# Feature group 1 of the gated branch by seven products on two chunks, and three moves around it

## The chip, the cores and the metric

The kernel runs on one core of one Trainium2 chip. The metric is the device time of one execution in microseconds. A core has five engines that each take their own list of instructions in order: PE (TensorE, matrix products into PSUM banks), ACT (ScalarE), DVE (VectorE), POOL (GpSimd) and SP (SyncE, which here only issues DMA transfers; ACT and POOL issue some too). The lists wait for each other through semaphores.

## The reference

Everything is float32. The input is 2048 positions of 640 features.

```python
xn = _layernorm(x)                        # over the 640 features
s = attention(xn)                         # 32 heads of 20; W = 8 keys at distances 0, 2, .., 14
g = silu(((xn @ w_gate) * (xn @ w_up)) @ w_down)     # 640 -> 1536 -> 640
return x + s * g
```

The attention takes q, k and v from xn @ wqkv (640 to 1920), masks keys before position 0, takes a softmax over the 8 keys and multiplies by wo (640 to 640).

## The kernel before, in words

**Products.** A float32 operand is split into a high part (a rounded copy, made by ACT, line 114) and a low part (the rest, a subtraction, line 115, on POOL or DVE), and a product is the sum of three: high by high, high by low, low by high. So 128 features against a chunk of 512 positions with 640 = 5 x 128 inputs takes 15 matmuls of 128x512.

**Gate and up.** The 1536 features are 12 groups of 128 (`f`), the 2048 positions 4 chunks of 512 (`ch`). For groups 0 and 1 the kernel does the plain thing, `gate_up(f, ch)` (line 642): 15 matmuls for gate, 15 for up, and DVE multiplies the two. For groups 2 to 10, `group(f, c0)` (line 1253) treats gate and up of two chunks (`c0`, `c0 + 1`) as a 2 by 2 block product and does it with seven block products (a scheme of Strassen's kind): 7 x 6 matmuls for four fifths of the inputs, and 4 x 3 plain ones for the last fifth. It needs sums of the weights (`w_add`: S1, S2, S3, S4, d5), their splits (`w_split`: sets G, S, R and U) and sums of the inputs (T1 to T4, made by `differences` for chunks 2 and 3, by `early_sums` and `early_high` for chunks 0 and 1).

Inside a group the products come in the order j = 0, 5, 2, 1, 4, 3, 6 (line 1285), here called n0 to n6. Products 0, 2, 4 and 6 add up in one PSUM bank (A), 1 and 3 in a second (C), 5 in a third (B). After j = 0, 1, 2 and 4 the running sum is copied out by ACT (`hold`, line 1261) before the next product adds to that bank. n0 and n1 read the weights of set G, n2 to n4 those of S (n3 also U), n5 those of R, n6 those of U.

**What is prepared when.** The raw weights of group f + 1 are loaded (`load_wf`, line 180, 640 KB) while group f runs, their sums and splits stand at places of group f (`places`, filled from `two_places`): for a full group of two halves (chunks 2 and 3, then 0 and 1) the sums at n5, n6 of the first half and n0, n1 of the second, the splits G, S, R, U at n2, n4, n5, n6 of the second half. The raw weights and the sums share two buffers (`wraw`), so that a load waits for the split that last reads the buffer.

**Order of the program.** A start stage (layer norm, transposes, q/k/v of the first head group for positions of both parities, `gate_up` of groups 0 and 1); then q/k/v of the other head groups m = 1 to 4, two times 8 tiles each (line 1356, `qkv`, PSUM copied out by ACT at line 448); then the groups; then wo, then w_down and the result. Attention's elementwise work (DVE: products L542 and L508, sums L549; POOL: the additions of L514; ACT: exponential L571 and a copy of q L498) is a generator that `advance(budget)` feeds piece by piece into the lists, at so many microseconds of credit per stretch of PE's work. In `values` (line 500) the eight weighted keys w = 0 to 7 of a unit go through two buffers in turn: the addition for w = 1 reads both, so the product for w = 2 has to wait for it. When a unit's additions are done, `store_o` (line 582) sends its result out on SP.

The number `VEC` decides on which engine the last additions of a group's first half are done (line 1257): DVE from group VEC on.

## Time and profile before

| what | value |
|---|---|
| runs | median 736.25 us of 3 (735.91 to 736.73) |
| the profiled execution: its time | 736.29 us |
| its span, first to last instruction | 734.4 us |
| PE busy | 728.2 us (99%) |
| DVE, POOL, ACT busy | 626.5 (85%), 450.5 (61%), 302.2 (41%) us |
| granted clock | 1.000 |

In the timelines a row holds its start, its length, engine, line, operation, what it writes and reads, and the count of equal instructions merged; in brackets stands the idle time ahead of it and who ended it. Times are from the span's start. A matmul row of PE reaches past the start of the next one, since matmuls overlap; the distance of starts tells what they cost.

### The profile page before, as it was taken

Reading aid. Unit: us, or ns where it says so; the run is one execution under the profiler, and the core shown is the slowest. Engines: PE = TensorE matmul, PEld = TensorE weight load, DVE = VectorE, ACT = ScalarE, POOL = GpSimd, SP = SyncE. Lnnn points to the kernel's source line nnn. Section 1 sums busy time; section 2 is a strip of 40 time slices with the busy share of each in tenths; the row PEclk is TensorE's granted clock in tenths of the full one; section 3 lists DMA queues with packets and bytes.
Section 4 is the critical chain, followed back from the end, with each engine's and each line's share of the span. In section 5 each row is a group of like instructions: output and inputs, shape, how many; then the busy total and the mean of one; then the engine's idle time right before and its main releaser. Section 6 shows DMA issues by size and latency. Waiting matters only on the chain.

```text
span 734.4 us, 11062 instructions
## 1 busy us (share of the span) xinstructions
PE 728.2 (99%) x4030; PEld 666.0 (91%) x4030; DVE 626.5 (85%) x729; ACT 302.2 (41%) x561; POOL 450.5 (61%) x383
## 2 busy tenths in 40 slices
PE   8999999999999999999999999999999999999997
PEld 6989989988999998888888888888999999999997
DVE  7676998798796989899889999969899997777775
ACT  5668312323232333333233322334566664444442
POOL 6159919997779889797879969766644550000000
PEclk9999999999999999999999999999999999999999
DMA  8564588789767669462733542376768965555534
GB/s 325 170 204 158 208 303 300 239 256 257 190 193 164 220 204 323 141 180 87 221 88 105 177 141 68 80 218 183 208 211 241 315 236 194 194 194 194 194 108 143
DMA packets 106148, 143.78 MB, mean 196 GB/s; under 512 B 23048, under 2 KB 75524, under 8 KB 106094
## 3 DMA queue, kind: packets, MB, share of 16 engines
q1 hardware_dynamic: 88366, 121.13, 52.0%
q10 hardware_dynamic: 16000, 12.78, 5.4%
q0 software_dynamic: 1728, 9.18, 5.1%
q8 instruction: 31, 0.51, 0.3%
q14 instruction: 23, 0.19, 0.1%
HBM read 94.40 MB, written 55.67 MB: 204 GB/s over the span
## 4 chain that ended last, share of the span: by engine, by line
PE 98%; DMA 1%; DVE 0%; SPq 0%; ACT 0%; issue 0%
PE g L1292 16%; PE u L1292 11%; PE q L434 11%; PE q L866 9%; PE u L434 8%; PE g L434 8%; PE u L866 6%; PE q L1292 5%; PE u L124 5%; PE g L124 5%; PE q L996 3%; PE g L866 3%; PE e L866 3%; PE u L996 2%; PE e L996 2%; PE g L996 1%
## 5 line engine op out<-in xcount | busy, mean ns | idle before, releaser
L514 POOL TENSOR_TENSOR o<-o,t 128x960 f32<-128x960 f32 (+1 forms) x66 | 133.7, 2025 | 11.3 <-DVE t L508 10.1
L508 DVE TENSOR_TENSOR t<-e,kv 128x960 f32<-128x960 f32 (+1 forms) x96 | 99.6, 1038 | 21.1 <-POOL o L514 21.1
L542 DVE TENSOR_TENSOR t<-q,kv 128x1920 f32<-128x1920 f32 (+1 forms) x48 | 92.4, 1926 | 2.8 <-DMA kv<-qkv_scr 2.7
L549 DVE TENSOR_REDUCE lg<-t 128x96 f32<-128x1920 f32 (+1 forms) x48 | 92.3, 1923 | 0.2
L434 PE MATMUL q<-s,xc 128*128 128x360 f32 (+1 forms) x450 | 82.8, 334 | 0.5 <-DVE lg L272 0.5
L1261 ACT ACTIVATE gh<-g 128x512 f32<-128x512 f32 x57 | 34.2, 600 | 109.0 <-PE g L1292 108.1
L434 PEld LDWEIGHTS q<-s,xc 128*128 128x128 f32 x450 | 74.8, 188 | 4.6 <-DVE lg L272 0.7
L115 POOL TENSOR_TENSOR s<-wraw,s 128x384 fp32r<-128x384 f32 (+6 forms) x57 | 68.0, 1209 | 17.5 <-ACT s L114 17.5
L434 PE MATMUL u<-s,xc 128*128 128x360 f32 (+1 forms) x360 | 65.8, 334 | 0.0
L434 PEld LDWEIGHTS u<-s,xc 128*128 128x128 f32 x360 | 60.3, 188 | 2.3
L434 PE MATMUL g<-s,xc 128*128 128x360 f32 (+1 forms) x330 | 61.5, 337 | 0.0
L434 PEld LDWEIGHTS g<-s,xc 128*128 128x128 f32 x330 | 55.7, 188 | 2.6
L1292 PE MATMUL g<-s,s 128*128 128x512 f32 x228 | 57.9, 389 | 0.0
L1292 PE MATMUL u<-xc,s 128*128 128x512 f32 x228 | 57.9, 389 | 0.0
L866 PE MATMUL q<-xc,s 128*128 128x320 f32 x342 | 55.5, 309 | 0.0
L866 PEld LDWEIGHTS q<-xc,s 128*128 128x128 f32 x342 | 51.5, 188 | 0.0
L1292 PEld LDWEIGHTS g<-s,s 128*128 128x128 f32 x228 | 42.8, 188 | 8.9
L1292 PEld LDWEIGHTS u<-xc,s 128*128 128x128 f32 x228 | 42.8, 188 | 8.9
L114 ACT ACTIVATE s<-wraw 128x384 fp32r<-128x384 f32 (+6 forms) x58 | 32.6, 581 | 29.4 <-PE g L1292 10.2
L1292 PE MATMUL q<-xc,pk 128*128 128x512 f32 x171 | 41.9, 389 | 0.0
L1292 PE MATMUL g<-xc,s 128*128 128x512 f32 x171 | 41.9, 389 | 0.0
L514 POOL TENSOR_TENSOR o<-t 128x960 f32<-128x960 f32 (+1 forms) x11 | 22.1, 2011 | 27.4 <-DVE t L508 22.7
(328 smaller groups left out, 1559.7 us busy)
## 6 DMA issues: line engine op xcount, KB each, us to landing
h_scr<-gh SPq DMA_DIRECT2D x48, 256.0 KB, 2.8
wraw<-in_wgu SPq DMA_DIRECT2D x11, 640.0 KB, 4.8
kv<-qkv_scr SPq DMA_DIRECT2D x14, 480.0 KB, 6.1
t<-h_scr SPq DMA_DIRECT2D x8, 768.0 KB, 6.3
qkv_scr<-s ACTq DMA_DIRECT2D x17, 360.0 KB, 4.4
kv<-qkv_scr SPq DMA_DIRECT2D x14, 367.5 KB, 7.1
s_scr<-gh SPq DMA_DIRECT2D x16, 320.0 KB, 3.6
gh<-s_scr SPq DMA_DIRECT2D x16, 320.0 KB, 4.1
```

The costliest lines, as they stand in the source:

```text
L114: nc.scalar.activation(hi, raw, AF.Copy)
L115: eng.tensor_sub(lo, raw, hi.bitcast(F32))
L124: nc.tensor.matmul(acc, a, b, start=first and n == 0, stop=last and n == len(runs) - 1)
L434: nc.tensor.matmul(p, xT[(r * NE + i) // TPC][a][:, k, t0:t0 + P], wq[m][b][k], start=n == 0, stop=n == len(runs) - 1, skip_group_check=ac ...
L508: nc.vector.tensor_mul(t.rearrange("p (n d) -> p n d", d=DH), e[:, :, w].unsqueeze(2).to_broadcast([P, NE * nh, DH]), v)
L514: return NE * c * cost, lambda: eng.tensor_add(y, z, t)
L542: nc.vector.tensor_mul(t, q, k)
L549: nc.vector.tensor_reduce(out=lg[:, :, j:j + 2].rearrange("p n a -> p a n"), in_=t.rearrange("p a (n d) -> p a n d", d=DH), op=ALU.add, ax ...
L866: nc.tensor.matmul(p, y[:, i, k], wd_part(name, k, l), start=new and r == 0, stop=r == len(runs) - 1, skip_group_check=True)
L996: nc.tensor.matmul(b, y, w, start=new and r == 0, stop=r == len(runs) - 1, skip_group_check=True)
L1261: nc.scalar.activation(kept[j], b["ACACABA"[j]], AF.Copy)
L1292: nc.tensor.matmul(y, w, x, start=j in (0, 1, 5) and r == 0, stop=r == len(runs) - 1, skip_group_check=True)
```

## The change

- `F_TWO` is 1: group 1 of chunks 2 and 3 goes through `group(1, 2)`, first of the groups, and the two plain calls `gate_up(1, 2)` and `gate_up(1, 3)` are gone. (Group 1 of chunks 0 and 1 stays plain.) The raw weights of group 1 are loaded a second time for it.
- This first group has only one half, so it has its own places (`one_places`), at which group 2 is prepared within that half. `VEC` is 1, the late loads of chunk 0 and 1's sums are spread differently, and a condition at n6 is widened.
- In the start stage the split of q/k/v weights 1, the load of weights 2 and `early_high(1)` stand after tile 5 of the second parity, in that order; `early_high(1)` came before the split, and the load of weights 2 at the start of m = 1.
- `store_o` stands after the exponential instead of ahead of the mask.
- The credit per head and tile in the q/k/v loop is 0.39 instead of 0.38.

```diff
-VEC = 2
+VEC = 1
...
             ahead(n + 1, (0,))
-            if before is not None:
-                store_o(before)
...
             finish_piece()
             yield 0.5
+            if before is not None:
+                store_o(before)
...
-    early_high(1)
...
     for i in range(TPC, NE):
         qkv(0, 1, i)
         advance(PACE * 1.9)
-    split_wq(1, nc.gpsimd)
-    gate_up(1, 2)
+        if i == TPC + 1:
+            split_wq(1, nc.gpsimd)
+            load_wq(2, ((0, 2), (2, 4)))
+            early_high(1)
     gate_up(0, 3)
-    gate_up(1, 3)
+    wf_raw.clear()
...
-    F_TWO = 2
+    F_TWO = 1
...
-            if (second, n) == (1, 6) and (second, n) in places:
+            if n == 6 and (second, n) in places and (second or f == F_TWO):
                 places.pop((second, n))(f)
...
-            advance(PACE * heads * 0.38)
+            advance(PACE * heads * 0.39)
...
-    w_split(2, "R")
-    w_sum.pop(2)
-    load_wf(3)
+    w_split(F_TWO, "R")
+    w_sum.pop(F_TWO)
+    load_wf(F_TWO + 1)
...
-    for f in range(2, f1):
+    one_places = {(0, 2): splits("G"), (0, 3): sums("S1", "S2", "S3"), (0, 4): splits("S"),
+                  (0, 5): lambda f: (w_add(f + 1, "d5", "S4"), w_split(f + 1, "R")), (0, 6): splits("U")}
+    for f in range(F_TWO, f1):
         places.clear()
-        places.update(two_places)
+        places.update(two_places if f > F_TWO else one_places)
         if f == F_TWO:
-            for n, at in enumerate((0, 2, 3, 4)):
+            places[0, 0] = lambda f: load_late(0)
+        elif f == F_TWO + 1:
+            for n, at in enumerate((0, 2, 4), 1):
                 places[0, at] = lambda f, n=n: load_late(n)
         group(f, 2)
-        group(f, 0, 1)
+        if f > F_TWO:
+            group(f, 0, 1)
```

ACT at the start of the groups, of the change. The first two rows split sets R and U of group 1 (`s_193`); `gh` rows are the holds; `wraw_194` is the raw weight tile of group 2, `wraw_201` its sums; `pk_190` is set G, `s_181` set S; the rows L569 and L498 belong to attention.

```order
L114 ACTIVATE s_193_2555<-wraw_172_2205 128x384 [waits Pool_49]
L114 ACTIVATE s_193_2555<-wraw_168_2141 128x384
L1262 ACTIVATE gh_197_2570<-g_195_2560 128x512 [waits PE_49]
L1262 ACTIVATE gh_199_2594<-g_195_2560 128x512 [waits PE_49]
L114 ACTIVATE pk_190_2501<-wraw_194_2558 128x640 [waits DMAHW6_49,Pool_49]
L1262 ACTIVATE gh_200_2609<-u_196_2561 128x512 [waits PE_49]
L1262 ACTIVATE gh_202_2623<-g_195_2560 128x512 [waits PE_49]
L114 ACTIVATE s_181_2368<-wraw_201_2611 128x768 [waits Pool_49]
L114 ACTIVATE s_193_2555<-wraw_201_2611 128x384 [waits PE_49,Activation_49,Pool_49]
L114 ACTIVATE s_193_2555<-wraw_194_2558 128x384 [waits PE_49,Activation_49]
L569 ACTIVATE e_3_70<-lg_188_2463 128x256 [waits DVE_49]
L498 ACTIVATE q2_2_69<-q_192_2549 128x640 [waits DMAHW0_49]
```

The same place before, from the split of R and U of its first group (group 2) on:

```order
L114 ACTIVATE s_202_2645<-wraw_182_2301 128x384 [waits Pool_49]
L114 ACTIVATE s_202_2645<-wraw_179_2235 128x384
L1261 ACTIVATE gh_206_2660<-g_204_2650 128x512 [waits PE_49]
L571 ACTIVATE e_3_70<-lg_191_2458 128x256 [waits DVE_49]
L498 ACTIVATE q2_2_69<-q_197_2552 128x640 [waits DMAHW7_49]
L1261 ACTIVATE gh_210_2687<-g_204_2650 128x512 [waits PE_49]
L1261 ACTIVATE gh_212_2701<-u_205_2651 128x512 [waits PE_49]
L1261 ACTIVATE gh_214_2713<-g_204_2650 128x512 [waits PE_49]
L1261 ACTIVATE gh_218_2757<-g_216_2749 128x512 [waits PE_49,Pool_49]
L1261 ACTIVATE gh_220_2790<-g_216_2749 128x512 [waits PE_49,Pool_49]
L114 ACTIVATE pk_199_2595<-wraw_203_2648 128x640 [waits DMAHW1_49,Pool_49]
```

The first split of the next group's weights (`pk` from the tile just loaded) stood behind six holds, and stands now behind two; the other three splits stand ahead of the next group's first hold.

POOL at the same place, of the change. `o_185` rows are attention's additions; the first row is the low part of set G of group 1, the two `s_193` rows those of R and U.

```order
L115 TENSOR_TENSOR pk_190_2501<-wraw_168_2141,pk_190_2501 128x640
L514 TENSOR_TENSOR o_185_2442<-t_77_926 128x640
L514 TENSOR_TENSOR o_185_2442<-o_185_2442,t_77_926 128x640 x2
L115 TENSOR_TENSOR s_193_2555<-wraw_172_2205,s_193_2555 128x384
L115 TENSOR_TENSOR s_193_2555<-wraw_168_2141,s_193_2555 128x384
L1149 DMA s_198_2572<-t_scr_111 128x1536
L514 TENSOR_TENSOR o_185_2442<-o_185_2442,t_77_926 128x640 x2
L115 TENSOR_TENSOR pk_190_2501<-wraw_194_2558,pk_190_2501 128x640
L1239 TENSOR_TENSOR wraw_201_2611<-wraw_194_2558 128x256
L1239 TENSOR_TENSOR wraw_201_2611<-wraw_201_2611,wraw_194_2558 128x256
L1239 TENSOR_TENSOR wraw_201_2611<-wraw_194_2558 128x256
L514 TENSOR_TENSOR o_185_2442<-o_185_2442,t_77_926 128x640
```

And before:

```order
L115 TENSOR_TENSOR pk_199_2595<-wraw_179_2235,pk_199_2595 128x640
L514 TENSOR_TENSOR o_189_2439<-o_189_2439,t_77_942 128x640 x3
L115 TENSOR_TENSOR s_202_2645<-wraw_182_2301,s_202_2645 128x384
L115 TENSOR_TENSOR s_202_2645<-wraw_179_2235,s_202_2645 128x384
```

The three additions between the splits were the last three of a unit (w = 5, 6, 7); now they are the first three of the next (w = 1, 2, 3; the row that writes `o` from `t` alone is w = 1). Behind them POOL now has the whole preparation of group 2 in a row: split G, three sums, an addition, split S (`s_181`), two sums, split R, an addition, split U.

On SP the load of group 2's raw weights, `wraw_194`, stands behind the loads of attention's next unit and waits for POOL's low part of R, which reads the buffer last; before, the load of group 3's weights waited for the same row of group 2.

14 lines of the change are left out of this document (7 added, 7 removed).

## The prediction

> **What bounds the kernel now.** I read the page's first part, then PE's waits, then the timelines of PE, ACT, POOL, DVE and SP where the groups begin.
>
> ```profile
> span 734.4 us, 11062 instructions
> PE 728.2 (99%) x4030; PEld 666.0 (91%) x4030; DVE 626.5 (85%) x729; ACT 302.2 (41%) x561; POOL 450.5 (61%) x383
> ...
> PE q L229 <- POOL lg masks.py:199: 1.4, 1, 1.4
> PE q L434 <- DVE lg L272: 0.5, 1, 0.5
> ```
>
> The last two rows are all the waits that PE has, and both lie in the start stage. From there on PE's matmuls alone set the time: a matmul less is time won, and any wait of PE is time lost, since nothing later is idle that could give it back.
>
> ```profile
> 85.00 3.56 PE L124 MATMUL g<-xc,s 128*128 128x512 f32 x15
> ...
> 105.40 2.56 PE L434 MATMUL q<-s,xc 128*128 128x360 f32 x15
> ...
> 272.60 1.52 PE L1292 MATMUL g<-xc,pk 128*128 128x512 f32 x6
> 273.96 2.20 PE L1292 MATMUL q<-xc,pk 128*128 128x512 f32 x9
> 276.00 1.52 PE L1292 MATMUL g<-s,s 128*128 128x512 f32 x6
> 277.36 1.52 PE L1292 MATMUL u<-s,s 128*128 128x512 f32 x6
> 278.72 0.84 PE L1292 MATMUL u<-xc,s 128*128 128x512 f32 x3
> 279.40 1.52 PE L1292 MATMUL g<-s,s 128*128 128x512 f32 x6
> 280.76 2.20 PE L1292 MATMUL u<-xc,s 128*128 128x512 f32 x9
> 282.80 2.20 PE L1292 MATMUL g<-xc,s 128*128 128x512 f32 x9
> 284.84 1.52 PE L1292 MATMUL g<-xc,pk 128*128 128x512 f32 x6
> ```
>
> From 85.00 to 105.40 stand three plain gate_up calls, 90 matmuls in 20.40 us, 0.227 us each. From 272.60 to 284.84 stands one half group, n0 to n6, 54 matmuls in 12.24 us, the same 0.227 us.
>
> **What is removed.** Two plain calls of 30 matmuls become one half group of 54: 6 matmuls, 6 x 0.227 = **1.36 us**. Were nothing else to happen, the profiled time of 736.29 us would become 734.93. All other work is on other engines, and costs only what PE comes to wait. So I look at the new half group, whose start on PE I call 0; in the run before, 0 is 272.60. Without waits n2 ends at 4.76, n3 at 6.80, n4 at 8.16, n6 at 12.24, and n1 of the group after it at 12.24 + 3.40 = 15.64.
>
> **What is added: one chain.** The change's lists show it. Group 2's raw weights can only be loaded when POOL has made the low part of R of group 1. ACT's split G of group 2 waits for that load and stands *ahead* of the hold of n3's bank, to which n5 adds; and the splits S, R and U stand ahead of the first hold of group 2, without which its n2 may not add. ACT starts its rows in the order of its list, so each hold waits for all that stands before it.
>
> When is R ready? These are the rows before, for the same place of the program (the first is the copy of the last head group's tile 13, 0.47 long after 1.93 of waiting for PE: a tile takes PE 2.40; all of this hangs on PE's position, so I shift it by 13.60 with PE).
>
> ```profile
> 268.00 0.47 ACT L448 ACTIVATE s<-g 128x360 f32<-128x360 f32 x1 [1.93 <-PE g L434]
> ...
> 269.07 0.74 ACT L114 ACTIVATE pk<-wraw 128x640 fp32r<-128x640 f32 x1 [0.60 <-ACT s L448]
> ...
> 273.87 0.94 ACT L114 ACTIVATE s<-wraw 128x384 fp32r<-128x384 f32 x2 [0.60 <-ACT s L448]
> 274.71 0.58 ACT L1261 ACTIVATE gh<-g 128x512 f32<-128x512 f32 x1
> 275.19 0.38 ACT L571 ACTIVATE e<-lg 128x256 f32<-128x256 f32 x1
> 275.50 0.70 ACT L498 ACTIVATE q<-q 128x640 f32<-128x640 f32 x1
> ...
> 259.91 1.56 POOL L514 TENSOR_TENSOR o<-t 128x640 f32<-128x640 f32 x1
> 262.42 1.57 POOL L514 TENSOR_TENSOR o<-o,t 128x640 f32<-128x640 f32 x1 [0.94 <-DVE t L508]
> ...
> 264.62 1.56 POOL L514 TENSOR_TENSOR o<-o,t 128x640 f32<-128x640 f32 x1
> ...
> 269.89 1.57 POOL L115 TENSOR_TENSOR pk<-wraw,pk 128x640 fp32r<-128x640 f32 x1 [1.59 <-ACT pk L114]
> 271.42 4.88 POOL L514 TENSOR_TENSOR o<-o,t 128x640 f32<-128x640 f32 x3
> 276.24 2.02 POOL L115 TENSOR_TENSOR s<-wraw,s 128x384 fp32r<-128x384 f32 x2
> ...
> 229.79 0.39 ACT L571 ACTIVATE e<-lg 128x256 f32<-128x256 f32 x1 [2.11 <-DVE lg L569]
> ...
> 261.51 0.82 DVE L508 TENSOR_TENSOR t<-e,kv 128x640 f32<-128x640 f32 x1 [1.70 <-POOL o L514]
> ...
> 277.30 0.35 SPq L180 DMA_DIRECT2D wraw<-in_wgu x1
> ```
>
> POOL's low part of G waited for ACT, hence for PE, and ended at 271.46, that is -1.14. Three additions followed back to back (4.88), then R, and SP issued the load at 277.30 = +4.70. The change has three additions in the same gap, so **+4.7 is the early bound** of the issue, T. But they are now w = 1, 2, 3, and w = 2's product may start only after w = 1's addition. The rows of such a trio are at 259.91, 262.42 and 264.62: with DVE's wait (261.51) and a 0.62 us DMA issue between them they took 6.27 us from the first start to the last end. From -1.14 that is +5.1, R takes 1.0, and T = **+6.2**. I take this, since it is the same trio; the late bound is DVE behind by the longest that ACT's exponential waited for it in the q/k/v loop's rows, 2.11 us (229.79), so +8.3.
>
> What then has to pass until group 2's first hold is done? The prices:
>
> ```profile
> DMA to landing us min/median/max: 4.5/4.5/4.5
> ...
> 283.34 0.73 POOL L1238 TENSOR_TENSOR wraw<-wraw 128x256 f32<-128x256 f32 x1
> 284.15 1.07 POOL L1238 TENSOR_TENSOR wraw<-wraw,wraw 128x256 f32<-128x256 f32 x1
> ...
> 286.97 1.61 POOL L1238 TENSOR_TENSOR wraw<-wraw 128x256 f32<-128x256 f32 x2
> 288.55 0.74 POOL L1238 TENSOR_TENSOR wraw<-wraw,wraw 128x256 f32<-128x256 f32 x1
> ...
> 293.06 1.56 POOL L514 TENSOR_TENSOR o<-o,t 128x640 f32<-128x640 f32 x1
> 294.61 1.85 POOL L115 TENSOR_TENSOR s<-wraw,s 128x768 fp32r<-128x768 f32 x1
> ```
>
> Landing 4.5 (the load at 277.30); split G, ACT's start to POOL's end, 271.46 - 269.07 = 2.4; S1, S2, S3: 0.8 + 0.8 + 0.8 = 2.4; the addition that POOL's list has ahead of split S 1.6; split S 1.85; d5 and S4 some 1.3; ACT's R and U 0.94; the exponential and the copy of q 1.0 (275.19 to 276.20); the hold 0.58. Sum **16.5**. The hold is done at T + 16.5 and PE wants it at 15.64, so PE loses T + 0.9: 5.6 at the early bound, **7.1** at +6.2, 9.2 at the late one. It is lost in two places: the hold of n3's bank ends at T + 4.5 + 0.74 + 0.58 = +12.0 against 8.16, some 3.9 us ahead of n5, and the other 3.2 us ahead of n2 of group 2.
>
> **The edits that I cost at nothing.** The added sums, splits and holds of group 1 itself lie in the q/k/v loop behind PE, as group 2's did. The earlier m = 1 (13.60 us) needs weights 1 split by 91.8 on PE:
>
> ```profile
> 80.61 1.30 POOL L608 TENSOR_TENSOR kv<-kv,xc 128x512 f32<-128x512 f32 x1
> ...
> 89.61 4.39 POOL L115 TENSOR_TENSOR s<-wraw,s 128x1080 fp32r<-128x1080 f32 x3
> ...
> 109.50 2.27 POOL L514 TENSOR_TENSOR o<-t 128x960 f32<-128x960 f32 x1 [14.80 <-DVE t L508]
> ```
>
> The split now follows POOL's 80.61 row and is done near 82 + 4.4 = 86.4; `early_high(1)`, between those rows at 7.7 us, comes after it and ends near 94, in what was POOL's idle 14.80 us. Without that cover it would delay the split to 94, and PE by about 2 us. It does delay SP: a q/k/v store now stands behind its stores, so attention's second unit starts some 4 us later (94 against 89.6 for the last of them). That costs DVE, not PE: ACT's copy of q waits for it and holds up five banks' worth of copies, 5 x 2.4 = 12 us. The moved `store_o` waits for POOL's addition as it did. The credit of 0.39 brings 26 x 16 x 0.01 = 4.2 us of attention forward, against 13.0 of credit that the two calls no longer give and 9.9 that the half group does; DVE's share by group 2 is as before within 1 us. Price of all these if wrong: 1 to 3 us of PE's time.
>
> **Forecast.** 736.29 - 1.36 + 7.1 = 742.0 us; the profiled time is 0.04 above the median, so it stands for both. Its own range goes by the bounds of T, 740.5 to 744.1.
>
> **Rivals.** *The load is early enough*, and the change does what its matmuls say: 734.9, a shade under 0.2% faster, which is about what a measurement of this kernel can tell from no change. It decides from T = -0.9 on. Against it: ACT's split of R, ahead of POOL's, waits in its list for the last tile's copy and started at 273.87 = +1.27. For it: only that I read the order of the holds right from lists, without times. *Only the first wait stays*, if POOL's sums are covered better than I count: 736.29 - 1.36 + 3.9 = 738.8. *The early stage costs too*: the late unit and its copy on ACT add 1 to 3 us, 743 to 745. *The clock falls after the pauses.* The granted clock is 1.000 here, with no wait of PE over 1.4 us, so no row shows what a 3 to 4 us pause does. If PE ran at half clock afterwards for as long as it paused, the first loss would vanish in the second wait, which does not hang on PE; the second would cost 3.2 / 2 = 1.6 us: 743.6.
>
> [...]
>
> **How the numbers follow.** Forecast 0.64, no wait 0.12, first wait only 0.08, early stage 0.08, clock 0.08. The range 737.0 to 746.5 takes in all but the no-wait case and the tails, about 0.82. Faster by over 0.2% is half of the no-wait case, 0.06; within 0.2% the other half and a little of the small waits, 0.08; slower 0.86.
>
> **What would show it.** PE's waits of the changed kernel should have ACT's holds (L1262) as releasers, some 4 us ahead of n5 and some 3 us ahead of n2 of group 2; the load of `wraw` should be issued some 6 us after the half group's start, and ACT should idle for DMA `wraw` ahead of split G. I am wrong if PE passes 259.0 to 275 without a wait, if T lies under 3, or if PE waits in m = 1.

## The result, and the profile after

The changed kernel takes **754.09 us** (median, 753.88 to 754.64) against 736.08 for the kernel before beside it: a ratio of 1.0245, 95% interval 1.0227 to 1.0262. It is 18 us slower. The prediction said 742.0, range 737.0 to 746.5: the direction was right, the size too small by 12 us. (One run of `b_36` and one of `b_wsum8`, its profiled one, took 1037.71 and 1037.48 us at a mean granted clock of 0.655, and stand in no number below.)

First the page of the changed kernel: its span, the busy time of the engines, and the first rows of PE's waits (engine, line, who was waited for: us in total, times, longest; the rest of them, 5.6 us, are in the places below or in the start stage).

```profile
span 752.0 us, 11077 instructions
PE 734.3 (98%) x4024; PEld 666.9 (89%) x4024; DVE 628.2 (84%) x731; ACT 305.4 (41%) x568; POOL 456.2 (61%) x392
...
PE u L1293 <- POOL s L115: 2.9, 2, 2.1
PE u L1293 <- ACT gh L1262: 2.7, 2, 2.0
PE g L1293 <- POOL pk L115: 2.1, 3, 1.4
```

Before, PE waited 1.9 us, all in the start stage. Now the new waits make some 11 us of the 17.6 by which the span grew, and PE is busy 6 us longer with 6 matmuls fewer. So part of the time is not waiting: PE itself was slower for a while. The starts of the first matmul of each stage give the whole account (a "half" is one half group, seven products; the column of differences adds up to the span's).

| stretch, us | before | after | difference |
|---|---|---|---|
| start to the first product of m = 1 | 105.40 | 91.81 | -13.6 |
| q/k/v loop, m = 1 to 4 | 167.20 | 170.98 | **+3.8** |
| half group 1 (new) | none | 20.07 | 12.24 **+ 7.8** |
| half group 2 | 12.24 | 13.43 | **+1.2** |
| half groups 3 to 20, over 12.24 each | 0 | 6.2 | **+6.2** |
| what follows the groups | 229.28 | 229.23 | 0 |

Saved 13.6 and spent 12.24 are the 1.36 us of the six matmuls. Against them stand 19.0 us in three places.

**The first half group.** PE, ACT, POOL and SP of the changed kernel, from each one's timeline:

```profile
262.79 1.19 PE L1293 MATMUL g<-xc,pk 128*128 128x512 f32 x4 [0.32 <-ACT pk L114]
...
272.57 0.50 PE L1293 MATMUL u<-xc,s 128*128 128x512 f32 x1 [2.14 <-POOL s L115]
276.71 4.21 PE L1293 MATMUL u<-xc,s 128*128 128x512 f32 x9 [1.98 <-ACT gh L1262]
280.71 2.31 PE L1293 MATMUL g<-xc,s 128*128 128x512 f32 x9
...
287.31 1.66 PE L1293 MATMUL g<-s,s 128*128 128x512 f32 x6 [0.89 <-ACT gh L1262]
```

```profile
262.00 0.74 ACT L114 ACTIVATE pk<-wraw 128x640 fp32r<-128x640 f32 x1 [3.95 <-DMA kv<-qkv_scr]
...
275.43 0.74 ACT L114 ACTIVATE pk<-wraw 128x640 fp32r<-128x640 f32 x1 [6.18 <-DMA wraw<-in_wgu]
276.07 0.58 ACT L1262 ACTIVATE gh<-u 128x512 f32<-128x512 f32 x1
...
264.34 1.56 POOL L514 TENSOR_TENSOR o<-t 128x640 f32<-128x640 f32 x1
266.85 1.57 POOL L514 TENSOR_TENSOR o<-o,t 128x640 f32<-128x640 f32 x1 [0.94 <-DVE t L508]
269.04 1.57 POOL L514 TENSOR_TENSOR o<-o,t 128x640 f32<-128x640 f32 x1 [0.62 <-DVE t L508]
270.56 1.95 POOL L115 TENSOR_TENSOR s<-wraw,s 128x384 fp32r<-128x384 f32 x2
...
271.58 0.35 SPq L180 DMA_DIRECT2D wraw<-in_wgu x1
```

This is the predicted chain. The trio of additions took 264.34 to 270.6, 6.3 us; the load of group 2's raw weights was issued at 271.58, 8.8 us after the start; ACT idled 6.18 us for it with the hold of n3's bank behind (276.07), and PE waited 1.98 us ahead of n5 (276.71). PE waited 0.89 more ahead of n2 of group 2. One wait is there that the prediction does not have: 2.14 us in n3 (272.57) for POOL's low part of U, the second of the two rows at 270.56, which stands behind the same trio and behind R. The load does not hang on it, so it does not move n5; but it is a pause of PE.

What no row of before could show is the row at 276.71: nine matmuls that take 4.0 us to the next start, where they took 2.04. The windows view shows why (stretch, length, PE busy and matmuls, granted clock, DMA share and GB/s):

```profile
270.62:274.03 3.41, 1.46 (x6) 1.00 0.38 113
274.03:277.44 3.41, 1.43 (x4) 0.50 0.83 283
277.44:280.86 3.42, 3.42 (x10) 0.50 0.09 32
```

The granted clock was 0.50 for 6.8 us, two stretches of 3.41, behind stretches in which PE worked 1.46 and 1.43 us of 3.41.

**The q/k/v loop.** The stretch around its one wait of PE, of PE, SP, POOL and ACT:

```profile
185.74 2.74 PE L434 MATMUL q<-s,xc 128*128 128x360 f32 x15 [0.96 <-ACT s L448]
...
254.91 2.63 PE L434 MATMUL g<-s,xc 128*128 128x360 f32 x15
257.38 2.63 PE L434 MATMUL u<-s,xc 128*128 128x360 f32 x15
...
167.59 1.51 SPq L422 DMA_DIRECT2D kv<-qkv_scr x2
169.27 0.34 SPq L414 DMA_DIRECT2D q<-qkv_scr x1
...
168.62 0.79 POOL L768 DMA_DIRECT2D w_scr<-w_scr x1
...
181.73 3.33 ACTq L452 DMA_DIRECT2D qkv_scr<-pk x2
185.11 0.57 ACT L448 ACTIVATE s<-q 128x480 f32<-128x480 f32 x1 [8.63 <-PE u L434]
```

ACT's store of q/k/v belongs right behind its copy at 175.9 and was issued at 181.73, which took 3.3 us; for 8.63 us ACT copied nothing out, and PE waited 0.96 us for its next copy. But the loop lost 3.8. The rest is in the two rows of PE below that wait: tiles of 360 columns start 2.47 us apart from here to the end of the loop, where before, and up to this wait, they started 2.40 apart. Thirty tiles make 2.1 us. Another 0.5 lies at the end of the loop, where the groups' first split comes late. The granted clock is 1.00 there.

**The later half groups** lose 0.1 to 2.0 us in five of them, by two kinds of wait. One of the first kind, at 391 us, from ACT's and PE's timelines, and one of the second, at 436 us, from POOL's and PE's:

```profile
391.24 0.50 ACT L569 ACTIVATE e<-lg 128x384 f32<-128x384 f32 x1 [1.77 <-DVE lg L567]
...
392.57 0.58 ACT L1262 ACTIVATE gh<-u 128x512 f32<-128x512 f32 x1
...
393.20 2.12 PE L1293 MATMUL u<-xc,s 128*128 128x512 f32 x8 [0.73 <-ACT gh L1262]
```

```profile
434.04 2.27 POOL L514 TENSOR_TENSOR o<-o,t 128x960 f32<-128x960 f32 x1
...
437.86 0.73 PE L1293 MATMUL g<-xc,pk 128*128 128x512 f32 x2 [1.44 <-POOL pk L115]
```

In the first, attention's exponential stands in ACT's list ahead of the hold that PE needs next, and it waited 1.77 us for DVE. In the second, one of attention's additions stands in POOL's list ahead of the low part of split G (from 436.27) that PE reads. By the releasers of PE's waits half groups 10 and 13, 2.4 us, are of the first kind, and 4 and 14, 3.7 us, of the second.

### The profile page after: what moved, and what is told of

Same layout as the page of the kernel before. It is cut to its first block, busy times and chain, and to the rows that moved or that the text cites. A ratio compares the mean times of both kernels' runs of the same rounds, so it can differ in the third digit from the quotient of the medians.

```text
span 752.0 us, 11077 instructions
## 1 busy us (share of the span) xinstructions
PE 734.3 (98%) x4024; PEld 666.9 (89%) x4024; DVE 628.2 (84%) x731; ACT 305.4 (41%) x568; POOL 456.2 (61%) x392
## 4 chain that ended last, share of the span: by engine, by line
PE 80%; DVE 6%; POOL 5%; issue 3%; DMA 3%; ACT 1%; SPq 0%; ACTq 0%; POOLq 0%; DVEq 0%
PE g L1293 10%; PE q L434 9%; PE q L866 8%; PE u L1293 7%; PE u L434 7%; PE g L434 6%; PE u L866 6%; PE u L124 4%; PE g L124 4%; PE q L1293 3%; PE q L996 3%; PE g L866 3%; PE e L866 3%; PE u L996 2%; POOL o L514 2%
## 5 line engine op out<-in xcount | busy, mean ns | idle before, releaser
L514 POOL TENSOR_TENSOR o<-o,t 128x960 f32<-128x960 f32 (+1 forms) x66 | 133.2, 2018 | 12.1 <-DVE t L508 11.2
L1262 ACT ACTIVATE gh<-g 128x512 f32<-128x512 f32 x60 | 35.9, 598 | 116.5 <-PE g L1293 114.9
L115 POOL TENSOR_TENSOR s<-wraw,s 128x384 fp32r<-128x384 f32 (+6 forms) x60 | 72.1, 1216 | 13.7 <-ACT s L114 13.7
L1293 PE MATMUL u<-xc,s 128*128 128x512 f32 x240 | 64.0, 402 | 5.6 <-POOL s L115 2.9
L1293 PE MATMUL g<-s,s 128*128 128x512 f32 x240 | 61.4, 391 | 0.9 <-ACT gh L1262 0.9
L1293 PEld LDWEIGHTS u<-xc,s 128*128 128x128 f32 x240 | 46.0, 193 | 18.0 <-ACT gh L1262 4.4
L1293 PEld LDWEIGHTS g<-s,s 128*128 128x128 f32 x240 | 45.0, 188 | 10.6 <-ACT gh L1262 1.3
L114 ACT ACTIVATE s<-wraw 128x384 fp32r<-128x384 f32 (+6 forms) x61 | 34.6, 584 | 43.3 <-PE g L1293 10.9
L1293 PE MATMUL g<-xc,s 128*128 128x512 f32 x180 | 44.3, 390 | 0.8 <-ACT gh L1262 0.8
L1293 PE MATMUL q<-xc,pk 128*128 128x512 f32 x180 | 44.2, 390 | 0.0
L1293 PEld LDWEIGHTS g<-xc,s 128*128 128x128 f32 x180 | 33.9, 189 | 8.4 <-ACT gh L1262 1.2
```

Source lines behind the costliest of these rows:

```text
L114: nc.scalar.activation(hi, raw, AF.Copy)
L115: eng.tensor_sub(lo, raw, hi.bitcast(F32))
L514: return NE * c * cost, lambda: eng.tensor_add(y, z, t)
L1262: nc.scalar.activation(kept[j], b["ACACABA"[j]], AF.Copy)
L1293: nc.tensor.matmul(y, w, x, start=j in (0, 1, 5) and r == 0, stop=r == len(runs) - 1, skip_group_check=True)
```

## The experiments

### Each of the four edits undone or done alone

In `no_store` the changed kernel has the store back ahead of the exponential:

```diff
             ahead(n + 1, (0,))
+            if before is not None:
+                store_o(before)
...
             yield 0.5
-            if before is not None:
-                store_o(before)
```

> The changed kernel with the store of attention's result back ahead of the mask and the exponential. Theory A: the q/k/v loop's extra 3.8 us (170.98 us from its first product to the first group's, against 167.20 before) come from the moved store, behind which SP now sends two units' loads in one burst while ACT's store of q/k/v waits; then the loop is back at 167.2 and the time falls from 754.1 to about 750. Theory B: the burst comes from q/k/v running 13.6 us earlier against attention, wherever the store stands; then the loop stays at about 171 and the time at 754 +- 1. In both the first half group still takes 18 to 20 us instead of 12.24, since its wait is for the weights' load.

`b_store` is the kernel before with only that store moved, the same lines the other way round.

> The kernel before with nothing but the store moved behind the exponential. Theory A (the store alone makes the burst): 739 to 740 us, with a wait of PE in the q/k/v loop. Theory B (the earlier q/k/v makes it): 736 +- 0.7 us, no new wait of PE.

`credit38`:

```diff
-            advance(PACE * heads * 0.39)
+            advance(PACE * heads * 0.38)
```

> The changed kernel with the credit 0.38 in the q/k/v loop, as before. Theory D: the waits after the first two half groups (6.2 us in six half groups) hang on where attention's exponential falls in the list ahead of a hold; 26 steps of 16 tiles x 0.01 move it by 4.2 us, and the late waits come out different by 2 us or more in sum. Theory E: they are a backlog of POOL and DVE from the first half group; then they stay at 5 to 7 us in sum, and the time at 753 to 755. The first half group stays at 18 to 20 us in both.

`no_early` has the early stage in its old order:

```diff
     low_parts()
+    early_high(1)
...
-        if i == TPC + 1:
-            split_wq(1, nc.gpsimd)
-            load_wq(2, ((0, 2), (2, 4)))
-            early_high(1)
+    split_wq(1, nc.gpsimd)
     gate_up(0, 3)
```

> The changed kernel with the early stage in its old order (the fifth set of sums of chunks 0 and 1 ahead of the split, the split of q/k/v weights 1 behind all tiles, the load of weights 2 at the start of m = 1). The prediction took the new order to cost nothing: then 754 +- 1. If the new order makes the late first unit and with it the burst of loads, the q/k/v loop falls from 171.0 towards 167.2 and the time to about 750. If the new order is what lets m = 1 start at 91.8 without a wait, as the prediction's cover says, PE waits some 2 us for the split before m = 1 and the time rises to about 756.

`only_group` is the kernel before with the group change alone: all three of these undone at once.

> The kernel before with group 1 by seven products alone: credit 0.38, the store ahead of the exponential and the early stage in its old order, with its calls of plain gate_up gone. The prediction's chain alone: 736.1 - 1.4 + 7 = 742. If the early stage's old order makes PE wait for the split of weights 1 at m = 1, as in the run that undid that order alone (0.75 us, and then a slower cadence of the 360-column products): 744 to 750. The late waits of 1 to 2 us each are expected here too, since the phase of attention against the groups is shifted.

| kernel | median, us (range) | ratio, 95% interval | q/k/v loop | half groups 1, 2, over 12.24 | the later ones, in sum |
|---|---|---|---|---|---|
| changed | 754.09 (753.88 to 754.64) | 1.0245, 1.0227 to 1.0262 | 170.98 | 7.8, 1.2 | 6.2 |
| `no_store` | 755.81 (755.33 to 757.78) | 1.0272, 1.0257 to 1.0288 | 171.07 | 6.0, 5.3 | 8.0 |
| `credit38` | 751.31 (745.24 to 752.19) | 1.0189, 1.0148 to 1.0229 | 167.20 | 4.1, 1.1 | 5.4 |
| `no_early` | 756.31 (755.29 to 756.82) | 1.0276, 1.0259 to 1.0294 | 172.36 | 7.9, 1.3 | 6.1 |
| `only_group` | 751.44 (747.82 to 754.39) | 1.0206, 1.0161 to 1.0250 | 171.91 | 1.6, 4.3 | 3.2 |
| `b_store` | 736.87 (736.13 to 738.05) | 1.0011, 1.0001 to 1.0020 | 167.20 | none, 1.1 | 0 |

(Median and ratio are of all runs, the last three columns of the profiled run. `b_store` has no half group 1; its 1.1 is in its second half group, a wait for one of POOL's loads.)

Theory A falls on both sides: the moved store costs 0.1% alone, and putting it back repairs nothing. The early stage's new order is worth some 2 us here, as its cover was meant to work; without it PE waits for the split of weights 1.

```profile
93.80 1.25 PE L434 MATMUL q<-s,xc 128*128 128x360 f32 x6 [0.48 <-POOL s L115]
94.89 2.63 PE L434 MATMUL g<-s,xc 128*128 128x360 f32 x15
97.36 2.63 PE L434 MATMUL u<-s,xc 128*128 128x360 f32 x15
```

Behind that wait too, in `no_early`, tiles of 360 columns start 2.47 apart, from here to 131.89 us. The wait is 0.48 us in this row, and 15 tiles by 0.07 us behind it are 1.0 more.

`credit38` has two faces: its profiled run (745.24) has no wait in the loop, its other three runs took 750.8 to 752.2. The kernels with 0.38 below all show the loop's wait in their profiles, so the credit is not what makes it; it is a near miss that falls either way. The three edits undone together leave 751.4: **the group change alone costs 15 us** (12 to 18 in its four runs), by all three of the places in the first table. Part of it is the wait for the split of weights 1, as in `no_early`, which the new order was to cover.

### What makes the wait in the q/k/v loop

At 168.62 POOL issues a transfer of 960 KB (`w_scr`), in the middle of two units' loads, the weights of m = 4 and the stores. Before, it was issued at 186.40, behind that crowd. `wsum` moves it there in the changed kernel:

```diff
-    W_SUMS = ((1, 2), (1, 12), (2, 4), (2, 12), (3, 7))
+    W_SUMS = ((1, 2), (1, 12), (2, 4), (3, 1), (3, 7))
```

> The changed kernel with one of the sums of w_down's blocks (a transfer of 960 KB that POOL issues, at tile 12 of m = 2, 168.6 us) moved behind the crowd of loads, to tile 1 of m = 3. Theory H (the q/k/v loop's 3.8 us come from transfers that share the DMA engines from 167 to 184 us: two units' loads, the weights of m = 4, q/k/v's stores and this sum; then ACT's store waits and PE's banks stay full): no wait of PE near 184, the loop takes 167.2 instead of 171.0, and the time falls from 754.1 to 750 +- 1. Theory I (ACT's store waits for a load on its semaphore whatever the crowd): the loop stays at 170 to 171.

`b_wsum8` does the reverse in the kernel before: `(2, 12)` becomes `(2, 8)`.

> The kernel before with the same sum moved the other way, from tile 12 to tile 8 of m = 2 (from 186.4 to about 173 us), onto its own crowd of loads at 170 to 181 us. Theory H: PE waits some 1 us near 190, and after it 480 or 360-column products run at the slower cadence (2.467 instead of 2.400 us a tile): 738 to 740 us. Theory I: 736 +- 0.7.

`wsum` took 751.48 us (751.36 to 752.25; ratio 1.0212, 1.0194 to 1.0230), the loop 168.64. The same place, ACT and PE:

```profile
176.94 1.20 ACTq L452 DMA_DIRECT2D qkv_scr<-pk x2
...
184.57 2.56 PE L434 MATMUL q<-s,xc 128*128 128x360 f32 x15
186.97 2.56 PE L434 MATMUL g<-s,xc 128*128 128x360 f32 x15
```

The store goes out at 176.94 instead of 181.73, PE does not wait, and the tiles stay 2.40 us apart. What is left of the loop's loss, 1.4 us, lies at its end, where ACT's split of G comes late. The transfer now goes out at 188.03; in the changed kernel, which issues it at 168.62, the DMA share is 0.91 to 1.09 in stretches of 2 us from 168 to 184. So theory H holds for the changed kernel, though time and loop came out 1.4 us longer than it expected. Its reverse does not: `b_wsum8` took 735.96 us (ratio 0.9999, 0.9989 to 1.0009), where H expected 738 to 740; only its times count. A crowd alone does not do it; in the kernel before the two units' loads start 8 us apart (170 and 178 us), in the changed one 2 us. That this comes from q/k/v being 13.6 us earlier, so that the next unit's data is ready when the unit before it is loaded, is argued and not shown.

### What sets the first two half groups: the late load, or POOL's work

`r_early38` is `credit38` with R of group 1 split three tiles before the end of the loop, ahead of G; `rl_early38` lists the load of group 2's weights there too:

```diff
             elif m == last and n == NT - 3:
+                w_split(F_TWO, "R")
+                w_sum.pop(F_TWO)
+                load_wf(F_TWO + 1)
                 w_split(F_TWO, "G")
...
     step(100)
-    w_split(F_TWO, "R")
-    w_sum.pop(F_TWO)
-    load_wf(F_TWO + 1)
```

> The changed kernel with credit 0.38 and the split of set R of group 1 three tiles earlier, ahead of split G, so that the load of group 2's raw weights need not wait for it behind three of attention's additions. Theory F (the chain from that load sets the first two half groups, as predicted: T + 0.9): the load is issued at about -1.6 instead of +5.45 us, the first half group takes 12.24 instead of 16.36, the clock does not fall, the second half group loses 0 to 1 us; 745.2 becomes about 741. Theory G (POOL's amount of work, 18 us of it in a half group of 12.24, sets it): the loss of 5.2 us in the two halves falls by at most 2 us, 743 to 745. If a run has the q/k/v loop's extra, 6 us more in each.

> The same, and the load of group 2's raw weights listed there too, ahead of attention's loads on SP. Theory F: issue at about -4, the first two half groups take 12.24 and at most 12.8, 740 to 741. Theory G: as in the run with R alone, within 1 us.

They took 751.05 (748.36 to 751.91) and 750.55 us (749.73 to 751.15), 1.0196 (1.0177 to 1.0216) and 1.0192 (1.0175 to 1.0209). Both profiles have the loop's wait again (172.1 and 173.0). The first half group lost 1.6 and 1.2 us instead of the 4.1 of `credit38`, the second 5.2 and 5.0 instead of 1.1. The load came at +0.4 us in `rl_early38`, later than hoped, since R's split on ACT stood behind the loop's late copies; even so the wait ahead of n5 was gone, and a longer one stood ahead of n2 of group 2. That left F and G both alive, and the next four tell them apart. All have the moved sum of `wsum` and the credit 0.39. "No attention" means:

```diff
-            advance(PACE * len(runs) * (GROUP_RATE if two(f) else 0.184))
+            if f != F_TWO:
+                advance(PACE * len(runs) * (GROUP_RATE if two(f) else 0.184))
```

`lite` has R and the load early and no attention in the first half group; `lite_late` no attention, and the load where the change has it.

> The changed kernel with that sum behind the crowd, R and the load of group 2's weights early, and no piece of attention listed in the first half group. Theory G (with the load early it is POOL's work in that half, some 9 us for group 2's preparation and 9 us of attention's additions, that makes the second half group wait): the wait of 3.1 us ahead of n2 of group 2 falls to 0 to 1.2 us, the clock does not fall, and the first two half groups lose 0 to 2 us in sum instead of 6.2. Theory J (the place of split G behind the hold of n2 on ACT sets it): it loses 3 us or more there still. Attention is 10 us later by this, so what is won may be lost behind the groups.

> The changed kernel with the sum of w_down's blocks behind the crowd and no piece of attention listed in the first half group; the load of group 2's weights stays late, behind R. Against the kernel with that sum moved alone (first two half groups 6.24 + 5.17 us over 12.24 each). Theory F (the load's chain, T + 0.9, sets the loss; attention in that half does nothing): the two lose 6 us or more in sum. Theory G (POOL's sum of work in that half): they lose 2 to 4 us, about as with the load early (2.70 + 1.09). Half groups 4 to 16: no wait over 0.4 us, as with attention left out of that half and the load early, if it is attention's place and lag that made them.

`best` has G, R and U split three tiles early, in this order, the load behind them, no attention in the first half group, and group 2's split G behind n1 instead of n2 (the sums move up by one product with it); `g_first` is `best` with attention in that half.

```diff
             elif m == last and n == NT - 3:
                 w_split(F_TWO, "G")
+                w_split(F_TWO, "R")
+                w_split(F_TWO, "U")
+                w_sum.pop(F_TWO)
+                load_wf(F_TWO + 1)
...
-    one_places = {(0, 2): splits("G"), (0, 3): sums("S1", "S2", "S3"), (0, 4): splits("S"),
+    one_places = {(0, 1): splits("G"), (0, 2): sums("S1", "S2", "S3"), (0, 4): splits("S"),
```

> The kernel with G, R, U and the load early and no attention in the first half group, with the credit per product back at 0.184 and group 2's split G one product earlier, behind n1 and ahead of the hold of n2. Theory D: with 0.184 the exponentials stand where they stood in the version that had no late wait, and the late waits of the version with 0.187 (7.8 us in half groups 5 to 17) fall to 0.4 us. The wait ahead of n2 of group 2: POOL's low part of G still stands behind three additions that end 8.1 us after the start, so 2 to 4.4 us with the clock. Attention's end costs 2.8 as before. 739 to 743.

> The same with attention listed in the first half group. Theory G (POOL's work there): two to four additions of 1.57 us between POOL's preparation rows make the second half group lose 2 to 4 us more than without them, and the later half groups wait again, as in the changed kernel (4 to 6 us in sum), since attention's places are those of the changed kernel. 744 to 750. Without an effect of the amount of work: as the other run there, within 1 us.

| kernel | load | attention in half 1 | median, us (range) | ratio, 95% interval | halves 1, 2 over 12.24 | sum |
|---|---|---|---|---|---|---|
| `wsum` | late | yes | 751.48 (751.36 to 752.25) | 1.0212, 1.0194 to 1.0230 | 6.2, 5.2 | 11.4 |
| `lite_late` | late | no | 748.96 (747.70 to 749.53) | 1.0177, 1.0160 to 1.0194 | 7.5, 0.3 | 7.8 |
| `lite` | early | no | 743.71 (742.35 to 743.96) | 1.0103, 1.0087 to 1.0119 | 2.7, 1.1 | 3.8 |
| `g_first` | early, with R and U | yes | 748.63 (748.07 to 749.43) | 1.0166, 1.0149 to 1.0183 | 0.1, 9.1 | 9.3 |
| `best` | early, with R and U | no | 743.51 (742.77 to 744.08) | 1.0098, 1.0083 to 1.0113 | 0.3, 4.2 | 4.4 |

Both are true, and of one size: the late load costs 4.0 us (`lite_late` less `lite`; a lower clock is part of it: its mean in the profiled run is 0.995 in `lite_late`, where the nine matmuls behind the wait for n3's hold took 3.57 us instead of 2.04, and 0.999 in `lite`), attention's rows in that half 3.6 with the load late (`wsum` less `lite_late`) and 4.8 with it early (`g_first` less `best`). ACT, POOL and PE of `best`, then ACT and PE of `g_first`, from split G of group 2 to its first hold:

```profile
264.81 0.74 ACT L114 ACTIVATE pk<-wraw 128x640 fp32r<-128x640 f32 x1 [3.48 <-DMA wraw<-in_wgu]
...
267.84 1.58 POOL L115 TENSOR_TENSOR pk<-wraw,pk 128x640 fp32r<-128x640 f32 x1
...
276.86 0.58 ACT L1262 ACTIVATE gh<-g 128x512 f32<-128x512 f32 x1
...
277.49 2.23 PE L1293 MATMUL g<-s,s 128*128 128x512 f32 x6 [2.26 <-ACT gh L1262]
```

```profile
264.88 0.74 ACT L114 ACTIVATE pk<-wraw 128x640 fp32r<-128x640 f32 x1 [3.36 <-DMA wraw<-in_wgu]
...
280.58 0.37 ACT L569 ACTIVATE e<-lg 128x256 f32<-128x256 f32 x1
...
281.52 0.57 ACT L1262 ACTIVATE gh<-g 128x512 f32<-128x512 f32 x1
...
282.14 2.07 PE L1293 MATMUL g<-s,s 128*128 128x512 f32 x4 [6.83 <-ACT gh L1262]
```

From split G to the end of the hold it is 12.6 us without attention's pieces in that half and 17.2 with them: three additions of 1.57 us on POOL in between, and the exponential ahead of the hold. The prediction's sum for the same stretch was 12.0. In `best` split G started at +5.6, when the load had landed, and the chain ended at +18.3; PE wants that hold at +15.64. **As it is prepared here, the first half group is too short for a whole group**: by 2.6 us without attention's pieces, by 7 with them. That it must be is not shown. In `best` POOL's low part of G (267.84) still stands behind three additions listed before the half group; in the kernel before it started 0.82 us after ACT's split, here 3.03, so 2.2 of the 12.6 us are theirs. Split G writes the one buffer (`pk`) that n0 and n1 of group 1 read until +3.4. With the load as early as can be and POOL free, the estimate from these rows is +3.4 + 10.4 = +13.8, in time for +15.64; no run has both.

### What makes the later waits: the place of attention's rows

`exp_late` is `rl_early38` with the exponential listed 1.5 us of credit later in the groups, the sum per unit kept:

```diff
-            yield 1.5
+            yield 3.0 if grouped else 1.5
             nc.scalar.activation(e, lg, AF.Exp, scale=SCALE)
...
-            yield 0.5
+            yield 0.2 if grouped else 0.5
...
-            yield 1.3
+            yield 0.1 if grouped else 1.3
```

> The kernel with R and the load early, and in the groups the exponential listed 1.5 us of credit later (the credit of a unit's tail is the same in sum: 3.0, 0.2 and 0.1 for 1.5, 0.5 and 1.3). Theory D (the late waits come from an exponential that waits for DVE and stands ahead of a hold): where the exponential moves behind the next hold, which is so for the last three to four units, the waits of 1.1 to 1.6 us at those places go or move; 1 to 3 us less than the kernel with R and the load early. Theory E (backlog): no difference over 0.7 us.

`gate` has the moved sum, R and the load early, and no exponential behind n1, n2 or n3:

```diff
             yield 1.5
+            while spot[0] in (1, 2, 3):
+                yield None
             nc.scalar.activation(e, lg, AF.Exp, scale=SCALE)
```

> The changed kernel with that sum behind the crowd, R and the load early, and a rule that in the groups no exponential is listed behind n1, n2 or n3 (it waits for n4, or stands behind n0), so that it never stands just ahead of a hold that PE needs soon. Theory D (an exponential that waits for DVE ahead of such a hold makes the late waits): the waits of half groups 4 and later fall from 4.5 to 6 us in sum to 0 to 2. Theory E (backlog of POOL and DVE): they stay over 3 us.

`b_39` and `b_36` are the kernel before with 0.39 and with 0.36 for 0.38, and nothing else. `lite2` is `best` with 0.187 instead of 0.184 of credit per product in the groups (and group 2's split G still behind n2).

> The kernel before with the credit 0.39 in the q/k/v loop, so that attention stands 4.2 us further at the first group and its exponentials fall at other places of the half groups. Theory D (the place of an exponential against the holds decides, and the kernel before has places that suit): waits of 1 to 2 us in some of the half groups, 737.5 to 741 us. Theory E (a lag of attention decides, and more credit lessens it): no wait, 736 +- 0.7.

> The kernel before with the credit 0.36, attention 8.4 us further back at the first group. Theory D: waits of 1 to 2 us in some half groups as with 0.39, at other places, 737.5 to 741. Theory E as prices go (less done by the loop is work that DVE and POOL, 92% and 83% busy in the groups, have to do there): waits at many half groups, POOL's splits among the releasers, 739 to 745, clearly more than with 0.39.

> The best version the runs point to: the sum behind the crowd; G, R and U of group 1 split in this order three tiles ahead of the groups and the load of group 2's weights behind them; no attention in the first half group, and 0.187 instead of 0.184 of credit per product in the later ones. If the waits of the version with attention left out (0.5 + 0.95 at G, 1.39 at U, 0.95 at the next half, 2.63 at attention's end) each go by what stood ahead of them in the lists: 737 to 740. It beats the kernel before, at 736.1, only if nothing is left of them but 1 us; I do not expect that.

| kernel | median, us (range) | ratio, 95% interval | half groups that lose over 0.3 us (number: us) |
|---|---|---|---|
| changed | 754.09 (753.88 to 754.64) | 1.0245, 1.0227 to 1.0262 | 4: 1.95, 10: 1.29, 13: 1.11, 14: 1.73 |
| `rl_early38` | 750.55 (749.73 to 751.15) | 1.0192, 1.0175 to 1.0209 | 4: 1.55, 7: 1.37, 16: 1.48 |
| `exp_late` | 752.76 (748.99 to 753.29) | 1.0215, 1.0190 to 1.0240 | 4: 1.45, 10: 0.64, 14: 0.83, 16: 3.07 |
| `gate` | 754.03 (753.47 to 754.31) | 1.0246, 1.0228 to 1.0264 | 6: 0.93, 10: 0.53, 12: 2.71, 14: 4.27 |
| `g_first` | 748.63 (748.07 to 749.43) | 1.0166, 1.0149 to 1.0183 | 4: 0.64, 10: 1.27, 13: 1.11, 14: 1.64 |
| `best` (0.184) | 743.51 (742.77 to 744.08) | 1.0098, 1.0083 to 1.0113 | 11: 0.33, 19: 2.76 |
| `lite2` (0.187) | 750.65 (746.78 to 752.23) | 1.0190, 1.0160 to 1.0220 | 5: 1.23, 10: 3.53, 11: 1.24, 14: 1.29, 17: 0.52, 19: 4.35 |
| `b_39` | 746.45 (745.26 to 748.19) | 1.0143, 1.0127 to 1.0159 | 2: 0.79, 10: 0.31, 11: 3.63, 12: 7.47 |
| `b_36` | 753.10 (750.70 to 753.71) | 1.0223, 1.0202 to 1.0244 | 1: 1.09, 4: 2.03, 9: 0.59, 10: 7.28, 13: 0.75, 18: 2.97 |

(In `b_39` and `b_36` half group 1 is the first of group 2. For the others the first two, which the section before is about, are left out: `exp_late` lost 2.1 and 5.2 us there, `gate` 2.7 and 7.6, `lite2` 0 and 4.4.) **The kernel before, with its credit changed by 0.01, loses 10 us**, where theory D expected 1.5 to 5 and E none. Its groups do the same work; only attention's rows stand at other places between theirs. ACT of `b_39` and PE's row, and then ACT of the kernel before at the same unit:

```profile
413.30 0.60 ACT L1261 ACTIVATE gh<-g 128x512 f32<-128x512 f32 x1 [4.47 <-PE g L1292]
421.49 0.49 ACT L571 ACTIVATE e<-lg 128x384 f32<-128x384 f32 x1 [7.59 <-DVE lg L569]
...
422.82 0.58 ACT L1261 ACTIVATE gh<-g 128x512 f32<-128x512 f32 x1
...
423.45 2.93 PE L1292 MATMUL g<-s,s 128*128 128x512 f32 x6 [4.74 <-ACT gh L1261]
```

```profile
415.60 0.60 ACT L1261 ACTIVATE gh<-g 128x512 f32<-128x512 f32 x1 [0.76 <-PE g L1292]
...
418.71 0.50 ACT L571 ACTIVATE e<-lg 128x384 f32<-128x384 f32 x1 [1.78 <-DVE lg L569]
...
421.04 0.60 ACT L1261 ACTIVATE gh<-g 128x512 f32<-128x512 f32 x1
```

Before, the exponential stands behind the hold of n4, and no hold is due for 5 us; its wait for DVE costs nothing. In `b_39` it stands between the holds of n0 and n2, waits 7.59 us, and PE waits 4.74 for the hold behind it. The same holds from the other side: `best` and `lite2` differ by 0.003 of credit per product (and by the place of one split in the first half), and the later half groups lose 3.2 us with the one and 12.2 with the other. And the changed kernel and `g_first`, with the same credit, lose at the same half groups 10, 13 and 14, 1.1 to 1.7 us each, though the first two half groups of the one lost 9.0 and of the other 9.3 at quite different points. Further, `lite` and `lite_late`, with attention some 10 us further back, lose at most 0.7 us in any of half groups 3 to 18. So theory D holds in this: the places decide. It is too narrow in another: not exponentials alone stand at bad places, but also additions ahead of POOL's splits, as in half group 11 of `b_39`, where PE waited 2.70 us for POOL's low part of G.

The lag has a part in the price, too. `wsum` has the same rows in the same order on ACT, POOL and DVE in the groups as the changed kernel, and half group 4 loses 0.04 us in the one and 1.95 in the other. `b_36`, with attention 8.4 us further back, loses more than `b_39` with it 4.2 us further on; an exponential that need not wait for DVE would cost nothing at a bad place. And D's cures failed: `exp_late` lost 6.0 us in the later half groups, `rl_early38` 4.5; and `gate`, which keeps the exponentials out of the bad places, loses 8.5 us there, now in waits for POOL's splits behind attention's additions. Perhaps holding attention back for a few products bunches its rows on POOL; no run tested that. How much of each wait is place and how much lag is not settled.

**No version beats the kernel before.** The nearest, `best` and `lite`, equal within their ranges, stay 1% behind; `best` loses 4.4 us in the first two half groups and 2.8 at attention's end (which it pushed 10 us back), against 1.36 won.

## Why the prediction was right or wrong

- **Six matmuls less, 1.36 us**: right. The stretch to m = 1 shrank by 13.6, and where nothing waited a half group took 12.24 (the first of `lite2`: 12.24).
- **The chain on which the forecast rests**: right in its links, with one left out. The load waits for R behind three additions that took 6.3 us as predicted (6.27), ACT's split G waits for the load with n3's hold behind it, and PE waits ahead of n5 and ahead of n2 of group 2. Left out was U: its low part ends a row after R's, so by the prediction's own numbers at +7.2, and n3 wants it at +6.6. Mis-sized was the chain's start: G's low part on POOL ended at +1.6 and not at -1.14, because ACT's split G came 0.79 us ahead of the half group and not 3.53 (262.00, after 3.95 us of idling behind a store that waited for attention's loads). So T was 8.8 where the prediction took 6.2 and had 8.3 as its bound. Its formula T + 0.9 gives 9.7; measured were 9.0.
- **"Prices at nothing" for the early edits**: right for the order of the early stage (undoing it costs 2 us) and for the store (0.1% alone). Wrong for what the early m = 1 does to the transfers: the cover that the prediction named, five banks of 2.4 us, was used up when a store of ACT waited 5 us in a crowd of transfers and ACT copied nothing for 8.63, and then the loop lost 3.8. The rival "early stage, 1 to 3 us" had the place wrong (the late first unit) and the size a little too small.
- **The step that failed** is the sentence that the credit leaves "DVE's share by group 2 ... as before within 1 us". As an amount that may hold. But the change moves the groups against attention's rows, and what counts is ahead of which hold an exponential stands, and ahead of which of POOL's splits an addition. Together with attention's lag that makes 6.2 us here (2.4 at holds, 3.7 at splits) and up to 17 in the kernel before with another credit. The prediction looked at places in the first two half groups only and priced the other eighteen at nothing. It should have looked at every exponential's and addition's place in the new list, or taken the absence of any wait in the kernel before as a sign that its places had been fitted to its credit.
- **The clock**: the rival had it as a case of its own at 743.6, with pauses of 3 to 4 us. It came, 6.8 us at 0.50, beside pauses of 2.14 and 1.98, and some 2.3 us of the 7.8 of the first half group are matmuls at that clock; as the rival said, much of it vanished in the wait that followed. That the clock is at half for as long as PE paused was its assumption, and no run shows it: the changed kernel had 6.83 us at 0.50, `best` 3.41 behind a pause of 2.26.
- The sum: 1.9 us too little for the chain, 3.8 for the loop, 6.2 for the later half groups make 11.9 of the 12.1 us by which 742.0 missed.

## What to carry to other kernels

Where lists are filled by a credit or a planner, a change of length in one stage moves every later row of the interleaved work: price the new places of the rows that wait (here an exponential ahead of a hold, an addition ahead of a split), not only the amounts, and test the kernel before with its credit moved a little, to see how much of its time hangs on places. A faster stage also moves transfers onto each other (here two units' loads start 2 us apart instead of 8), and an engine that issues transfers stands still with its other work when one of them has to wait (here ACT copied nothing for 8.63 us). Work that is prepared one unit ahead needs a unit as long as its chain, with whatever else stands in the chain's lists: halving the first unit leaves the chain whole.

## What the runs showed of the hardware that was not expected

**A granted clock of 0.50 for 3.41 and for 6.83 us.** In the changed kernel the granted clock is 0.50 from 274.03 on for 6.83 us, and again from 751.90, behind PE's last product, to the end of the record; the two begin 477.87 us apart, which is 140 times 3.413. Cut into stretches of 3.41 us from 270.62 on, one in which PE worked 1.46 us is followed there by one at 0.50, this one, with 1.43 us of work, by another at 0.50, and that one, with 3.42, by one at 1.00. The same cut of `best`, whose PE paused 2.26 us, and then of `wsum`, where it paused 2.2 and 2.6 us (in each row: length, PE, PEld, DVE, ACT and POOL busy, then the clock, DMA share and GB/s; where the stretches of `wsum` begin, whose clock does not change in them, is an estimate):

```profile
274.91:278.32 3.41, 1.15 (x6) 0.70 (x5) 1.95 (x4) 1.42 (x3) 2.78 (x4) 1.00 0.13 37
278.32:281.73 3.41, 3.41 (x10) 2.64 (x9) 2.25 (x3) 0.60 (x1) 3.31 (x4) 0.50 0.80 232
281.73:285.15 3.42, 3.42 (x17) 2.81 (x16) 3.10 (x5) 1.42 (x3) 3.40 (x5) 1.00 0.91 277
```

```profile
266.12:269.53 3.41, 1.89 (x9) 1.23 (x7) 3.41 (x4) 0.60 (x1) 2.88 (x3) 1.00 0.00 0
269.53:272.95 3.42, 1.89 (x7) 1.24 (x7) 3.42 (x5) 0.00 (x0) 3.32 (x4) 1.00 0.82 224
272.95:276.36 3.41, 1.72 (x7) 1.43 (x8) 3.38 (x5) 1.71 (x3) 3.09 (x3) 1.00 0.54 198
276.36:279.77 3.41, 3.41 (x16) 2.82 (x15) 2.52 (x6) 0.85 (x1) 3.33 (x4) 1.00 0.02 5
```

In `best` the pause stands within one stretch, with 1.15 us of work, and the next, at 0.50, has 10 matmuls where the one behind it has 17. In `wsum` the two pauses are spread over three, with 1.89, 1.89 and 1.72 us of work, and the clock stays at 1.00. So of pauses of 2 to 3 us these runs show some with half clock behind them and some without; what decides it is not shown.

**A slower cadence after a wait.** In the q/k/v loop of the changed kernel tiles of 360 columns start 2.40 us apart up to PE's wait of 0.96 us ahead of 185.74, and 2.47 (2.8% more) from 188.31 to the groups, at a granted clock of 1.00. In `no_early` they start 2.47 apart behind a wait of 0.48 us (93.80), from 94.89 to 131.89, where tiles of 480 columns come; these start 3.25 apart there, and 3.25 in the changed kernel, where PE has not waited in the loop by then. Where PE did not wait in the loop the tiles of 360 are 2.40 apart: in the kernel before (from 105.40 to 143.80 and from 195.80 to 272.60), in `wsum` at the same place (182.17 to 198.97) and at the end of the loop of `credit38` (253.88 to 258.68). What makes the difference of 0.07 us a tile no run shows.
